# Gates of the first two chunks by seven half-size products, on fp16 sums kept in borrowed space

## The chip, the core and the metric

One core of one Trainium2 chip runs the whole program. The metric is device microseconds (us) of one execution, as the median of several. Engines are named as in the profile: PE (TensorE matmuls), PEld (its weight loads), DVE (VectorE), ACT (ScalarE), POOL (GpSimd), SPq (the queue that issues most transfers).

## The reference, cut to what matters

```python
xn = _layernorm(x)                       # x: 2048 x 448
s  = attention(xn, k_cache, v_cache, wq, wo)          # 16 heads of 256, window 512
g  = silu((gelu(xn @ w_gate) * (xn @ w_up)) @ w_down) # F = 1792; this is the "gate"
out = x + s * g
```

The rows are handled in four chunks of 512. The products with w_gate and w_up (the FFN stage) of all chunks come first, in rounds of two units; a unit is 128 of the 1792 columns F, so a chunk has 14 units and 7 rounds, and "round n" computes units n and n + 1. The product with w_down of a chunk, followed by the silu, is called the gate of that chunk. Only the gates of chunks 0 and 1 lie within the FFN stage; the other two run later, among the attention scores.

## The kernel before: the parts concerned

```python
def gu_evac(n, b):                       # after the matmuls of unit n
    act(gl[:, s, :], bank[b], ACT.Gelu_apprx_tanh, ...)
    K.op("dve", tensor_tensor(actT[:, c % 2, f, :], bank[b + 1], gl[:, s, :], ALU.mult), ...)

def down(c, pairs):                      # the gate of chunk c: eight products
    for t4 in range(4):
        mms([(bank[b][:, 0:D], actT[:, c % 2, f, t4*P:(t4+1)*P], wd[:, f, :], f == 0, f == NF-1)
             for f in range(NF)], ...)
        act(tmp[:, s, 0:D], bank[b][:, 0:D], ACT.Tanh, ..., scale=0.5)
        K.op("dve", ... out=g2w[:, t % NXR, :] ...)     # NXR = 3 buffers
        dma("sp", g2d[t], g2w[:, t % NXR, :], ...)

def ln_norm(t, dup="dve"):
    nm(0, D, 0, b_xn[s][0])              # the 448 columns, on DVE
    if dup == "dve":
        nm(D, DP, K3, b_xn[s][1])        # the last 64 columns once more, on DVE
    else:
        act(xn[:, s, D:DP], xn[:, s, K3:D], ACT.Copy, ...)   # or copied, on ACT

def ln_a(): ...                          # statistics of the next tile (DVE), deviation (POOL)
def ln_b(): ln_norm(ln_t[1]); ln_tp_dma(ln_t[1]); ...

DOWN_AT = {NF + 5: 0, 2 * NF + 1: 1}     # gates of chunks 0 and 1
for n in range(4, NU, 2):                # the rounds
    gu_group((n, n + 1), cur)            # PE
    gu_evac(n, cur[0])
    ln_b()
    gu_evac(n + 1, cur[1])
    if ln_t[0] < 8 or n >= 12: ln_a()
    # ... casts and sums of wo, loads of wq, v, k at n == 32 ...
    if n + 1 in DOWN_AT: down(DOWN_AT[n + 1], cur)
```

VectorE and ScalarE each work through their own list in the order in which the program names the operations (the lines of round 18 below show it: a gelu whose bank was written by 39.52 us started at 42.78, behind the copy named before it). A round writes four PSUM banks and the next round the other four, so PE can start round n + 4 only when the products of round n have been read out (round 22 below waits 0.94 us for one of round 18).

The softmax here doesn't subtract the row's maximum and nothing guards it: scores larger than these inputs give would overflow.

## Time and profile before

| | before |
|---|---|
| median (later 4 runs) | 548.0 us (547.84 to 548.5) |
| PE busy | 98% of the span |
| gate of chunk 0, chunk 1 | 10.70 us each |
| PE idle behind the second gate | 1.23 us |
| one round | 3.02 us |

The prediction below shows the lines of the profile. In its timeline lines the columns are start in us, length in us, engine, source line, operation, output<-inputs, shapes, count, and in brackets the idle time before it with what ended that.

### The profile page before, as it was taken

What the parts mean: (1) busy time and instruction counts of PE and PEld (TensorE: products, weight loads), DVE (VectorE), ACT (ScalarE), POOL (GpSimd) and SP (SyncE); (2) the same over time, 40 slices, a digit from 0 to 9 for tenths busy, and PEclk for the clock granted to TensorE, in tenths of its full rate; (3) what the DMA queues carried; (4) which work ended last, traced back from release to release, by engine and by line L of the source; (5) the groups of instructions that cost most, each with busy time, mean ns of one, the idle gap of its engine ahead of it and who ended that gap; (6) DMA issues with size and microseconds to landing.
All of it is one profiled execution on the core that took longest, in us unless ns stands there. A gap on an engine that the chain in (4) does not pass through costs nothing.

```text
span 545.9 us, 10453 instructions
## 1 busy us (share of the span) xinstructions
PE 537.6 (98%) x3955; PEld 294.5 (54%) x3980; DVE 350.0 (64%) x785; ACT 305.1 (56%) x770; POOL 38.6 (7%) x78
## 2 busy tenths in 40 slices
PE   9999999999999999999999999999999999999997
PEld 5554444445444444894444459644444884444487
DVE  6673726673356757943875786367667934776775
ACT  5433625854448858305875860388578206876820
POOL 1130400000000000003001000020000003001010
PEclk9999999999999999999999999999999999999999
DMA  9568389922264827401771780057546402863731
GB/s 294 122 188 127 65 174 314 206 54 72 74 104 96 151 62 138 95 2 48 168 151 46 151 158 1 18 138 145 104 89 151 79 2 68 165 153 83 151 53 34
DMA packets 171458, 61.34 MB, mean 112 GB/s; under 512 B 154960, under 2 KB 168272, under 8 KB 171408
## 3 DMA queue, kind: packets, MB, share of 16 engines
q1 hardware_dynamic: 167632, 51.39, 44.2%
q0 software_dynamic: 3008, 8.72, 6.6%
q8 instruction: 31, 0.51, 0.4%
q10 hardware_dynamic: 768, 0.57, 0.3%
q14 instruction: 19, 0.16, 0.1%
HBM read 19.76 MB, written 3.67 MB: 43 GB/s over the span
## 4 chain that ended last, share of the span: by engine, by line
PE 93%; DMA 2%; ACT 2%; DVE 2%; issue 1%; DVEq 0%; ACTq 0%
PE bank L357 92%; DMA g_all<-g2w 2%; ACT p L703 1%; PE bank L474 1%; DVE pn L710 1%; ACT qT L348 0%; DVE rden L707 0%; DVE g2w L534 0%; PE bank L455 0%; DVE qT L688 0%; ACT oTh L348 0%; ACT xnT L348 0%; DVE xnT L351 0%; DVE xr L351 0%; DVE gl L387 0%
## 5 line engine op out<-in xcount | busy, mean ns | idle before, releaser
L703 ACT ACTIVATE p<-bank 128x512 f32<-128x512 f32 x256 | 150.5, 596 | 24.3 <-DVE pn L710 19.1
L357 PE MATMUL bank<-pT,va 128*128 128x512 bf16 x512 | 120.8, 379 | 0.0
L357 PE MATMUL bank<-kT,qT 128*128 128x512 bf16 x487 | 117.8, 379 | 2.3 <-ACT qT L348 1.0
L710 DVE TENSOR_SCALAR pn<-p,rden 128x512 bf16<-128x512 f32 x256 | 113.0, 484 | 7.8 <-DMA pT<-pn 3.6
L357 PE MATMUL bank<-xnT,wq 64*128 64x512 bf16 x768 | 94.9, 376 | 0.0
L357 PE MATMUL bank<-xnT,wgu 64*128 64x512 bf16 (+2 forms) x768 | 83.9, 350 | 1.3 <-DVE g2w L534 1.2
L357 PEld LDWEIGHTS bank<-kT,qT 128*128 128x128 bf16 x512 | 49.4, 98 | 62.0 <-issue 3.8
L357 PEld LDWEIGHTS bank<-pT,va 128*128 128x128 bf16 x512 | 50.0, 98 | 60.4 <-DMA pT<-pn 0.9
L348 ACT ACTIVATE qT<-bank 128x512 bf16<-128x512 f32 x76 | 44.1, 596 | 55.4 <-PE bank L357 53.8
L688 DVE CAST qT<-bank 128x512 bf16<-128x512 f32 x52 | 35.1, 692 | 54.7 <-PE bank L357 54.7
L357 PEld LDWEIGHTS bank<-xnT,wq 64*128 64x128 bf16 x768 | 36.7, 94 | 46.3 <-ACT p L703 2.1
L357 PEld LDWEIGHTS bank<-xnT,wgu 64*128 64x128 bf16 x768 | 37.0, 94 | 38.5 <-DVE g2w L534 1.7
L348 ACT ACTIVATE gl<-bank 128x512 bf16<-128x512 f32 x56 | 33.2, 597 | 39.0 <-PE bank L357 36.7
L707 DVE RECIPROCAL rden<-rsum 128x2 f32<-128x2 f32 x128 | 21.2, 166 | 49.6 <-ACT p L703 49.6
L523 DVE TENSOR_TENSOR actT<-bank,gl 128x512 bf16<-128x512 f32 x56 | 37.8, 690 | 21.9 <-PE bank L357 15.6
L703 ACT ACTIVATION_READ_ACCUMULATOR p<-bank 128x1 f32 x256 | 51.7, 202 | 0.0
L357 PE MATMUL bank<-wt,sr 128*128 128x224 f16 x512 | 49.7, 259 | 0.0
L357 PEld LDWEIGHTS bank<-wt,sr 128*128 128x128 f16 x512 | 49.1, 98 | 0.0
L348 ACT ACTIVATE xnT<-bank 128x224 bf16<-128x224 f32 (+2 forms) x12 | 4.4, 400 | 71.7 <-PE bank L357 70.9
L357 PE MATMUL bank<-wd,actT 128*128 128x448 bf16 x224 | 43.0, 353 | 0.0
L728 DVE TENSOR_SCALAR oTh<-bank 128x512 f16<-128x512 f32 x62 | 42.4, 684 | 0.0
L348 ACT ACTIVATE oTh<-bank 128x512 f16<-128x512 f32 x66 | 38.9, 590 | 4.6 <-PE bank L357 4.6
(51 smaller groups left out, 352.1 us busy)
## 6 DMA issues: line engine op xcount, KB each, us to landing
wtb<-in_A_wo_dram POOLq DMA_DIRECT2D x4, 896.0 KB, 10.8
wq<-in_A_wq_dram SPq DMA_DIRECT2D x2, 1536.0 KB, 9.2
va<-in_A_v_cache_dram SPq DMA_DIRECT2D x8, 256.0 KB, 6.3
pT<-pn SPq DMA_TRANSPOSE x128, 2.8
g_all<-g2w SPq DMA_DIRECT2D x16, 112.0 KB, 1.8
xr<-in_A_x_dram POOLq DMA_DIRECT2D x15, 112.0 KB, 2.4
wd<-in_B_w_down_dram SPq DMA_DIRECT2D x1, 1568.0 KB, 7.6
g<-g_all POOLq DMA_DIRECT2D x14, 112.0 KB, 2.3
```

Of the source, the lines that this page charges most:

```text
L348: K.op("act", lambda e, o=o, i=i: e.activation(o, i, func, scale=scale), reads, writes)
L357: ins = e.matmul(o, lhsT=l, rhs=r, start=st, stop=sp, skip_group_check=True)
L474: ins = e.matmul(bank[b][:, 0:w], lhsT=gl[:, 0, 0:P], rhs=gl[:, 0, 0:w], start=True, stop=True)
L523: K.op("dve", lambda e: e.tensor_tensor(actT[:, c % 2, f, :], bank[b + 1], gl[:, s, :], ALU.mult), (b_ps[b + 1], b_gl[s]), (b_actT[c % 2][ ...
L688: K.op("dve", lambda v, s=s, b=b: v.tensor_copy(qT[:, s, 1, :], bank[b + 1]), (b_ps[b + 1],), (b_qT[s][1],))
L703: K.op("act", lambda e, b=b, r=r, z=z: e.activation(p32[:, z, :], bank[b], ACT.Exp, scale=att_scale, accum_out=rsum[:, r:r + 1]), (b_ps[b] ...
L707: K.op("dve", lambda e, r=r: e.reciprocal(rden[:, r - 1:r + 1], rsum[:, r - 1:r + 1]), b_rsum[r - 1:r + 1], b_rden[r - 1:r + 1])
L710: K.op("dve", lambda e, r=r - 1 + t, z=(n - 1 + t) % NP32, y=y, t=t: e.tensor_scalar(pn[:, y, t, :], p32[:, z, :], rden[:, r:r + 1], None, ...
L728: K.op("dve", lambda v, i=i, b=b: v.tensor_scalar(oTh[:, i, :], bank[b], WS, None, op0=ALU.mult), (b_ps[b],), (b_oT[i],))
```

## The change

Its intent: in the gates of chunks 0 and 1, cut the matrices into 2 x 2 blocks and replace the eight products of blocks by seven (Strassen's scheme in Winograd's form), paying with sums of w_down and of the activations on DVE and casts to fp16 on ACT. The sums live in space that k, v and wq need later, so those loads move behind the second gate. The first gate moves from behind round 18 to behind round 26, the second from behind round 28 to behind round 38, and the layernorm of tiles 12 to 15 and the casts and sums of wo to later rounds. In every round with a layernorm, the copy of the last 64 columns moves from VectorE to ScalarE (`"act"`), where it stands between the two gelus. The core of the diff (the seven products and their sums are cut):

```diff
-        b_va = [K.buf() for g in range(Hkv)]
+        b_va = sbuf_bufs(a, NJ * Dh * 2, Hkv)
...
+        g2w = [g2w[:, i, :] for i in range(NXR)] + [g2[:, 0, :]]
+        b_g2w = sbuf_bufs(a, D * 2, NXR) + b_g2[:1]
...
+        wdt, b_wdt, a2 = temp("wdt", [P, 7, NH, N2], F16, b_kT[0].lo, 7)
+        sd, b_sd, a2 = temp("sd", [P, 4, NH, HC], F16, a2, 4)
...
+        def cast_wd(j, e, n, i): ...      # act: w_down to fp16
+        def sum_wd(o, x, y): ...          # dve: 128 x 1568
+        def sum_act(c, k, i): ...         # dve: 128 x 1024 or 128 x 768
+        def down7(c, one, other): ...     # seven products of 14 matmuls, 224 columns
...
         def ln_b():
             if ln_t[1] < ln_t[0]:
-                ln_norm(ln_t[1])
+                ln_norm(ln_t[1], "act")
...
-        DOWN_AT = {NF + 5: 0, 2 * NF + 1: 1}
+        WD_CASTS = [(16, (j, e, n, i)) for j, e, n in (...) for i in range(2)]
+        DN_SUMS = [(n, sum_act, (0, k, i)) for i, n in ((0, 14), (1, 16)) for k in range(4)] + [
+            (20, sum_wd, x) for x in (...)] + [
+            (n, sum_act, (1, k, i)) for i, n in ((0, 28), (1, 30)) for k in range(4)]
+        DOWN_AT = {27: 0, 39: 1}
...
-            if ln_t[0] < 8 or n >= 12:
+            if ln_t[0] < 8 or 12 <= n and ln_t[0] < 12 or n >= 28:
                 ln_a()
...
-            if n == 32:                   # loads of wq, v, k
...
+                cur, nxt = down7(DOWN_AT[n + 1], cur, nxt)
+                if DOWN_AT[n + 1] == 1:   # loads of wq(0), k 0-1, wq(1), v, k 2-7
```

More of the change, by code (lines that the diff above doesn't have):

```diff
@@ L270, in bass_recurrent_scan__sliding_block_cached__geglu_ffn__prompt_kernel @@
         g2w, _, _ = place("g2w", [P, NXR, D], BF16, at=a)
-        b_g2w = sbuf_bufs(a, D * 2, NXR)
+        g2w = [g2w[:, i, :] for i in range(NXR)] + [g2[:, 0, :]]
+        b_g2w = sbuf_bufs(a, D * 2, NXR) + b_g2[:1]
         tmp, a, _ = place("tmp", [P, 2, QC], F32)
@@ L301, in bass_recurrent_scan__sliding_block_cached__geglu_ffn__prompt_kernel @@
         b_actT = [sbuf_bufs(a + i * NF * QC * 2, QC * 2, NF) for i in range(2)]
+        actTh, _, _ = place("actTh", [P, 2, NF, QC], F16, at=a)
         NGL = 3
@@ L304, in bass_recurrent_scan__sliding_block_cached__geglu_ffn__prompt_kernel, with temp @@
         b_gl = sbuf_bufs(a, QC * 2, NGL)
+        NH = NF // 2
+        b_dn = []
+        def temp(name, shape, dt, at, n):
+            t, a, a2 = place(name, shape, dt, at=at)
+            b = sbuf_bufs(a, (a2 - a) // n, n)
+            b_dn.extend(b)
+            return t, b, a2
+        wdt, b_wdt, a2 = temp("wdt", [P, 7, NH, N2], F16, b_kT[0].lo, 7)
+        sd, b_sd, a2 = temp("sd", [P, 4, NH, HC], F16, a2, 4)
+        cd, b_cd, a2 = temp("cd", [P, 3, D], F32, a2, 3)
+        th, b_th, a2 = temp("th", [P, 2, D], F32, a2, 2)
+        g2x, a, a2 = place("g2x", [P, 4, D], BF16, at=at)
+        b_g2x = sbuf_bufs(a, D * 2, 4)
         NPT, NPN, NP32 = 3, 3, 3
@@ L522, in gu_evac @@
             act(gl[:, s, :], bank[b], ACT.Gelu_apprx_tanh, (b_ps[b],), (b_gl[s],))
-            K.op("dve", lambda e: e.tensor_tensor(actT[:, c % 2, f, :], bank[b + 1], gl[:, s, :], ALU.mult),
+            o = actTh if c < 2 else actT
+            K.op("dve", lambda e: e.tensor_tensor(o[:, c % 2, f, :], bank[b + 1], gl[:, s, :], ALU.mult),
                  (b_ps[b + 1], b_gl[s]), (b_actT[c % 2][f],))
@@ L533, in down @@
                 act(tmp[:, s, 0:D], bank[b][:, 0:D], ACT.Tanh, (b_ps[b],), (b_tmp[s],), scale=0.5)
-                K.op("dve", lambda e, t=t, b=b, s=s: e.scalar_tensor_tensor(
-                    out=g2w[:, t % NXR, :], in0=tmp[:, s, 0:D], scalar=1.0, in1=bank[b][:, 0:D],
-                    op0=ALU.add, op1=ALU.mult), (b_tmp[s], b_ps[b]), (b_g2w[t % NXR],))
-                dma("sp", g2d[t], g2w[:, t % NXR, :], (b_g2w[t % NXR],), (b_g2d[t],))
+                K.op("dve", lambda e, t4=t4, b=b, s=s: e.scalar_tensor_tensor(
+                    out=g2w[t4], in0=tmp[:, s, 0:D], scalar=1.0, in1=bank[b][:, 0:D],
+                    op0=ALU.add, op1=ALU.mult), (b_tmp[s], b_ps[b]), (b_g2w[t4],))
@@ new lines, in down, with cast_wd, sum_wd, sum_act @@
+                dma("sp", g2d[t], g2w[t4], (b_g2w[t4],), (b_g2d[t],))
+        def cast_wd(j, e, n, i):
+            fs = (slice(0, 4), slice(4, NH))[i]
+            fe = slice(e * NH + fs.start, e * NH + fs.stop)
+            act(wdt[:, j, fs, :], wd[:, fe, n * N2:(n + 1) * N2], ACT.Copy, (b_wd,), b_wdt[j:j + 1], scale=WS)
+        def sum_wd(o, x, y):
+            add("dve", wdt[:, o, :, :], wdt[:, x, :, :], wdt[:, y, :, :], [b_wdt[x], b_wdt[y]], b_wdt[o:o + 1], ALU.subtract)
+        def sum_act(c, k, i):
+            fs = (slice(0, 4), slice(4, NH))[i]
+            o = lambda e, r: (actTh[:, c, e * NH + fs.start:e * NH + fs.stop, r * HC:(r + 1) * HC],
+                              b_actT[c][e * NH + fs.start:e * NH + fs.stop])
+            S = lambda j: (sd[:, j, fs, :], b_sd[j:j + 1])
+            j, (x, bx), (y, by), op = ((3, o(0, 0), o(0, 1), ALU.subtract), (2, o(1, 1), S(3), ALU.subtract),
+                                       (0, S(2), o(0, 0), ALU.add), (1, o(1, 0), S(2), ALU.subtract))[k]
+            add("dve", S(j)[0], x, y, bx + by, S(j)[1], op)
@@ new lines, in down7, with product, plus, gate @@
+        def down7(c, one, other):
+            B1, B4, B6, B7, B5, B3 = one[0], one[0] + 1, one[1], one[1] + 1, other[0], other[0] + 1
+            F = 1.0 / WS
+            A = lambda e, r: (lambda i: actTh[:, c, e * NH + i, r * HC:(r + 1) * HC], b_actT[c][e * NH:(e + 1) * NH])
+            S = lambda i: (lambda k: sd[:, i, k, :], b_sd[i:i + 1])
+            U2, U3 = tmp[:, 0, 0:D], tmp[:, 1, 0:D]
+            bU2, bU3 = b_tmp[:1], b_tmp[1:]
+            def product(j, b, x, first=True):
+                lhs, bx = x
+                mms([(bank[b][:, t * N2:(t + 1) * N2], lhs(i)[:, t * P:(t + 1) * P], wdt[:, j, i, :],
+                      first and i == 0 and t == 0, False) for i in range(NH) for t in range(2)], bx + [b_wdt[j]], (b_ps[b],))
+            def plus(o, bo, b, V, bV):
+                K.op("dve", lambda e: e.scalar_tensor_tensor(
+                    out=o, in0=bank[b][:, 0:D], scalar=F, in1=V, op0=ALU.mult, op1=ALU.add), [b_ps[b]] + bV, bo)
+            def gate(q, r, n):
+                two = lambda x: x.rearrange("p (t d) -> p t d", t=2)
+                act(th[:, q % 2, :], cd[:, q % 3, :], ACT.Tanh, b_cd[q % 3:q % 3 + 1], b_th[q % 2:q % 2 + 1], scale=0.5)
+                def end():
+                    K.op("dve", lambda e: e.scalar_tensor_tensor(
+                        out=g2x[:, 2 * r:2 * r + 2, n * N2:(n + 1) * N2], in0=two(th[:, q % 2, :]), scalar=1.0,
+                        in1=two(cd[:, q % 3, :]), op0=ALU.add, op1=ALU.mult),
+                        (b_th[q % 2], b_cd[q % 3]), b_g2x[2 * r:2 * r + 2])
+                return end
+            def store(r):
+                for t in range(2 * r, 2 * r + 2):
+                    dma("sp", g2d[c * 4 + t], g2x[:, t, :], (b_g2x[t],), (b_g2d[c * 4 + t],))
+            product(0, B1, A(0, 0))
+            act(U2, bank[B1][:, 0:D], ACT.Copy, (b_ps[B1],), bU2, scale=F)
+            product(5, B6, S(2))
+            product(6, B7, S(3))
+            product(3, B4, A(1, 1))
+            product(4, B5, S(0))
+            product(2, B3, S(1))
+            product(1, B1, A(1, 0), False)
+            plus(U2, bU2, B6, U2, bU2)
+            plus(U3, bU3, B7, U2, bU2)
+            plus(cd[:, 0, :], b_cd[:1], B4, U3, bU3)
+            g0 = gate(0, 1, 0)
+            plus(cd[:, 1, :], b_cd[1:2], B5, U3, bU3)
+            g1 = gate(1, 1, 1)
+            plus(U2, bU2, B5, U2, bU2)
+            g0()
+            plus(cd[:, 2, :], b_cd[2:], B3, U2, bU2)
+            g1()
+            store(1)
+            g2_ = gate(2, 0, 1)
+            act(cd[:, 0, :], bank[B1][:, 0:D], ACT.Copy, (b_ps[B1],), b_cd[:1], scale=F)
+            g2_()
+            gate(3, 0, 0)()
+            store(0)
+            return (other[1], one[1]), (one[0], other[0])
@@ L625, in sum_wt @@
                 [b_wt[x][i], b_wt[y][i]], b_wt[o][i:i + 1], ALU.subtract)
-        CASTS = [(18, (j, i)) for j in (0, 4) for i in range(NB)] + [(40, (j, i)) for j in (2, 1) for i in range(NB)]
-        SUMS = [(32, (4, 4, 0, i)) for i in range(NB)] + [
-            (44, (o, x, y, i)) for i in range(NB) for o, x, y in ((5, 2, 4), (6, 5, 0), (3, 1, 5))]
-        DOWN_AT = {NF + 5: 0, 2 * NF + 1: 1}
+        CASTS = [(24, (j, i)) for j in (0, 4) for i in range(NB)] + [(46, (j, i)) for i in range(NB) for j in (2, 1)]
+        SUMS = [(40, (4, 4, 0, i)) for i in range(NB)] + [
+            (48, (o, x, y, i)) for i in range(NB) for o, x, y in ((5, 2, 4), (6, 5, 0), (3, 1, 5))]
+        WD_CASTS = [(16, (j, e, n, i)) for j, e, n in ((0, 0, 0), (4, 0, 1), (2, 1, 1), (1, 1, 0)) for i in range(2)]
+        DN_SUMS = [(n, sum_act, (0, k, i)) for i, n in ((0, 14), (1, 16)) for k in range(4)] + [
+            (20, sum_wd, x) for x in ((4, 4, 0), (5, 2, 4), (6, 5, 0), (3, 1, 5))] + [
+            (n, sum_act, (1, k, i)) for i, n in ((0, 28), (1, 30)) for k in range(4)]
+        DOWN_AT = {27: 0, 39: 1}
         gu_evac(0, 0)
@@ L652, in bass_recurrent_scan__sliding_block_cached__geglu_ffn__prompt_kernel @@
                 load_wt(4, 0, 1)
-            if n == 30:
+            if n == 36:
                 K.reuse([b for j in (1, 2, 3, 5, 6) for b in b_wt[j]])
@@ L656, in bass_recurrent_scan__sliding_block_cached__geglu_ffn__prompt_kernel @@
                 load_wt(1, 1, 0)
+            for i in range(2):
+                if WD_CASTS and n >= WD_CASTS[0][0]:
+                    cast_wd(*WD_CASTS.pop(0)[1])
+            for i in range(2 if n in (14, 20, 22, 24, 26, 36, 38) else 1):
+                if DN_SUMS and n >= DN_SUMS[0][0]:
+                    _, f, x = DN_SUMS.pop(0)
+                    f(*x)
             for i in range(2 if n >= 40 else 1):
@@ L659, in bass_recurrent_scan__sliding_block_cached__geglu_ffn__prompt_kernel @@
                     cast_wt(*CASTS.pop(0)[1])
-            for i in range(2 if n >= 44 else 1):
+            for i in range(3 if n >= 48 else 1):
                 if SUMS and n >= SUMS[0][0]:
                     sum_wt(*SUMS.pop(0)[1])
-            if n == 32:
-                for g in range(NG):
-                    load_wq(g)
-                for g in range(Hkv):
-                    load_v(g)
-                for g in range(Hkv):
-                    load_k(g)
-            if n + 1 in DOWN_AT:
-                down(DOWN_AT[n + 1], cur)
-                cur, nxt = nxt, cur
+            if n + 1 in DOWN_AT:
+                assert not DN_SUMS or DN_SUMS[0][0] > n
+                cur, nxt = down7(DOWN_AT[n + 1], cur, nxt)
+                if DOWN_AT[n + 1] == 1:
+                    K.reuse(b_kT + b_va)
+                    for b in [y for x in b_wql for y in x]:
+                        b.old.extend(y for x in b_dn for y in x.readers + [x.writer] if y is not None)
+                    load_wq(0)
+                    for g in range(2):
+                        load_k(g)
+                    load_wq(1)
+                    for g in range(Hkv):
+                        load_v(g)
+                    for g in range(2, Hkv):
+                        load_k(g)
         def q_group(n, pairs, more_act=False):
```

## The prediction

> **What bounds the kernel now.** I read the page's busy shares first, then the chain that ended last, then the groups, and last the timeline around the two gates (the products with w_down of chunks 0 and 1) that the change rewrites.
>
> ```profile
> PE 537.6 (98%) x3955; PEld 294.5 (54%) x3980; DVE 350.0 (64%) x785; ACT 305.1 (56%) x770; POOL 38.6 (7%) x78
> ...
> PE 93%; DMA 2%; ACT 2%; DVE 2%; issue 1%; DVEq 0%; ACTq 0%
> ```
>
> PE is busy 98% and carries 93% of the chain, so only two things move the end: matmul time taken out, and idle time of PE put in or taken out. From the timeline of the early stage, the second gate, and from the last burst, which already works with seven products (columns: start, length, engine, line, operation, count, idle before and its releaser):
>
> ```profile
> 63.89 10.77 PE L357 MATMUL bank<-wd,actT 128*128 128x448 bf16 x56
> ...
> 74.59 0.82 PE L357 MATMUL bank<-xnT,wgu 64*128 64x512 bf16 x6
> ...
> 79.20 0.62 DVE L534 SCALAR_TENSOR_TENSOR g2w<-tmp,bank 128x448 bf16<-128x448 f32 x1 [5.84 <-DMA g_all<-g2w]
> ...
> 79.88 0.82 PE L357 MATMUL bank<-xnT,wgu 64*128 64x512 bf16 x6 [1.23 <-DVE g2w L534]
> ```
> ```profile
> 524.09 12.43 PE L357 MATMUL bank<-wt,sr 128*128 128x224 f16 x128
> 536.36 6.30 PE L357 MATMUL bank<-wt,oTh 128*128 128x224 f16 x64
> ```
>
> A gate of eight products takes 74.59 - 63.89 = 10.70 us, 191 ns for each of 56 matmuls. A 224-column matmul of the seven-product kind goes at (536.36 - 524.09)/128 = 95.9 ns. And PE stood still 1.23 us because the last gate step waited for a buffer whose store was slow.
>
> How VectorE and ScalarE follow the FFN matmuls is the other half. One round is two units, and PE needs 3.02 us for it: VectorE's first products of successive rounds start at 20.00 and 23.03 below.
>
> ```profile
> 20.00 0.69 DVE L523 TENSOR_TENSOR actT<-bank,gl 128x512 bf16<-128x512 f32 x1 [0.47 <-PE bank L357]
> 20.61 0.60 DVE L430 TENSOR_SCALAR xn<-x,mv,rstd 128x448 bf16<-128x448 bf16 x2
> 21.12 0.69 DVE L523 TENSOR_TENSOR actT<-bank,gl 128x512 bf16<-128x512 f32 x1
> 21.72 0.62 DVE L404 BATCH_NORM_STATS2 stats<-x 128x6 f32<-128x448 bf16 x1
> 22.38 0.18 DVE L407 BATCH_NORM_AGGREGATE mv<-stats 128x2 f32<-128x6 f32 x1
> 23.03 0.69 DVE L523 TENSOR_TENSOR actT<-bank,gl 128x512 bf16<-128x512 f32 x1 [0.47 <-PE bank L357]
> ```
> ```profile
> L348 ACT ACTIVATE gl<-bank 128x512 bf16<-128x512 f32 x56 | 33.2, 597 | 39.0 <-PE bank L357 36.7 <-DVE stats L404 0.6
> L348 ACT ACTIVATE wt<-wtb 128x896 f16<-128x896 bf16 x16 | 14.7, 942 | 5.6 <-DMA wtb<-in_A_wo_dram 5.6
> L351 DVE TENSOR_TENSOR wt<-wt 128x896 f16<-128x896 f16 x16 | 9.5, 618 | 0.1
> L351 DVE TENSOR_TENSOR sr<-oTh 128x1024 f16<-128x1024 f16 x16 | 10.9, 684 | 0.0
> L430 DVE TENSOR_SCALAR xn<-x,mv,rstd 128x448 bf16<-128x448 bf16 x16 | 6.3, 392 | 0.7 <-POOL rstd L416 0.6
> L348 ACT ACTIVATE xn<-xn 128x64 bf16<-128x64 bf16 x1 | 0.3, 258 | 0.0
> ```
>
> A round with layernorm work leaves VectorE 0.47 us free. The last six lines are the by-shape groups (count, then busy us and mean ns): they price each new operation.
>
> [...]
>
> **The change part by part.**
> 1. *Products.* Chunks 0 and 1 take 7 x 7 x 2 = 98 matmuls of 224 columns instead of 56 of 448: 98 x 95.9 = 9.40 us against 10.70. Saved on PE: 1.30 each, 2.60 in all.
> 2. *Buffers of the gate.* Four own output buffers, and the large loads are issued after the second gate's stores: the stall of 1.23 us goes. Sum of gains: 3.83 us.
> 3. *Loads of wq, k, v.* They start some 2.5 us after the second gate ends, when the last use of the borrowed space is over, instead of at 80.2. Eight rounds (24 us) then pass before the first q product. In the kernel before, the whole sequence was issued in 30 us (80.2 to 110.7); wq's first half, k 0 and k 1 come first in the new order, and v 0 and k 2 are needed tens of us later. I count no stall.
> 4. *New side work.* ScalarE: eight casts of w_down (four of 942 ns, four of 672 elements[...]), two in each of rounds 16, 18, 20, 22: 1.6 us per round with overlap. VectorE: four sums of w_down of 1568 elements (slope (684-618)/128 = 0.52 ns, so 0.97 us each, estimate), and per chunk four sums of 1024 elements (0.69) and four of 768 (estimate 0.55). All of this is beside PE if the rounds stay under 3.02 us.
> 5. *The small copy of the normalized tile goes to ScalarE.* It now stands between the two gelus of a round. It waits for VectorE's normalization, which stands behind the product of the first gelu. So in a round with a normalization the two engines no longer run side by side: gelu 0.60, hand-over 0.07, product 0.61 (start to start, 20.00 to 20.61), normalization 0.39, hand-over 0.06, copy 0.26, gelu 0.60 = 2.59 us. VectorE saves little: both small steps together had taken 21.12 - 20.61 = 0.51.
>
> **The rounds against 3.02 us.** For ScalarE a round with copy and two casts is 2.59 + 1.6 = 4.2. For VectorE, from its first product to its next: 0.61 + 0.39 + (0.06 + 0.26 + 0.60 + 0.07) + 0.61 + statistics 0.84 + one sum 0.69 = 4.1. Round 14, with two dependent sums (1.4), is 4.8; rounds 16 and 18 are 4.2; round 20 is 4.2 by ScalarE. Together 17.4 us where PE needs 12.1: 5.3 late. A product may be late by 3.02 + 0.26 - 0.95 or so before PE misses its bank (it frees the bank 0.95 us after the round; the bank is wanted 3.02 after): 2.1 us of slack. So about 3.3 us of PE idle before the first gate, in rounds 20 to 26. Round 24 (products 1.24 and two large sums 2.0) keeps the lag: VectorE starts round 26 about 2.2 us late, and the sum for the third product is done 0.26 + 2.2 + 1.24 + 0.97 = 4.7 us after the gate starts, wanted at 2 x 1.34 = 2.7: 2.0 us more. First gate: 5.3.
> Chunk 1: rounds 30, 32, 34 are 4.1 by VectorE, 36 is 0.61 + 0.39 + 0.99 + 0.61 + 1.1 = 3.7: 16.0 against 12.1, 3.9 late, 2.1 slack, so about 1.5 of PE idle before the gate, and the second product then waits for the last act sums, about 1.7 more. Second gate: 3.2.
> Sum: -3.8 + 5.3 + 3.2 = +4.7 us, so 552.6.
>
> **Rivals.**
> - *The side work hides* and PE gains all 3.8 us: 544.0. For it: on averages both engines have room, and without the copy's hand-over ScalarE would need 1.2 + 1.6 = 2.8 us per round. Against: the order of the instructions in the built kernel, gelu, copy, gelu, with the copy waiting on VectorE. About one in five.
> - *Half hides*: the lag is smaller than my hand walk says, for instance because back-to-back operations overlap more. Then 546 to 550.
> - *The late loads become the bound*: q or the first scores wait for wq or k, or the score transposes queue behind the loads. Load issue took 30 us and 30 us are there before the first scores; each us over it costs up to 1 us. Then 555 to 560. Against: the order puts first what is needed first. One in fifteen.
>
> **Range and chances.** The sum is 552.6; the errors lie more on the low side (the first two rivals), so I say 551.6, with 545.8 to 555.0. More than 2% faster would need 11 us, three times the whole gain: 1%. More than 2% slower would need stalls of 15 us: 3%.
>
> **What would show it.** Matmuls of 224 columns in the gates at 96 ns: step 1. No wait of PE on the gate's store: step 2. PE idle of 3 to 4 us between rounds 20 and 26 put down to VectorE's product, then idle inside the first gate at its second and third product, released by a sum of w_down: step 5 and the walk. In ScalarE's waits a new row, the small copy waiting for the normalization, about 1.1 us each time. PE over 98% busy before 95 us would prove me wrong; so would idle at the first q product or the first scores (step 3).

## More of the kernel before

One further line is wanted later, the first product of the attention scores, as a mark that stands just behind the FFN stage:

```profile
121.65 1.67 PE L357 MATMUL bank<-kT,qT 128*128 128x512 bf16 x7 [0.16 <-DVE qT L688]
```

## The result, and the profile after

The changed kernel took 551.84 us (median of 4 runs, 551.44 to 553.04) against 548.01 before. The ratio is 1.0072, 95% interval 1.0054 to 1.009. The change costs 0.7%, well clear of the noise but under 2%.

The page's busy shares and its chain by engine, after:

```profile
PE 536.6 (98%) x4039; PEld 299.6 (55%) x4064; DVE 366.9 (67%) x805; ACT 313.2 (57%) x794; POOL 41.7 (8%) x78
...
PE 86%; DVE 5%; ACT 5%; issue 2%; POOL 1%; DMA 1%; DVEq 0%; ACTq 0%
```

PE is still busy 98%, rounded; but the chain that ended last, 93% PE before, now runs through DVE and ACT for a tenth of the span (4% before). The averages hide the change of regime; the chain shows it. The timeline of one round (round 18) shows how the two engines are tied together:

```profile
40.61 0.59 ACT L365 ACTIVATE gl<-bank 128x512 bf16<-128x512 f32 x1
...
41.30 0.69 DVE L541 TENSOR_TENSOR actTh<-bank,gl 128x512 f16<-128x512 f32 x1
...
42.19 0.40 DVE L447 TENSOR_SCALAR xn<-x,mv,rstd 128x448 bf16<-128x448 bf16 x1 [0.20 <-POOL rstd L433]
42.62 0.26 ACT L365 ACTIVATE xn<-xn 128x64 bf16<-128x64 bf16 x1 [1.42 <-DVE xn L447]
...
43.26 1.59 ACT L365 ACTIVATE wdt<-wd 128x896 f16<-128x896 bf16 x2
43.46 0.69 DVE L541 TENSOR_TENSOR actTh<-bank,gl 128x512 f16<-128x512 f32 x1 [0.88 <-ACT gl L365]
...
44.21 0.82 PE L374 MATMUL bank<-xnT,wgu 64*128 64x512 bf16 x6 [0.94 <-DVE actTh L541]
...
44.75 0.59 ACT L365 ACTIVATE gl<-bank 128x512 bf16<-128x512 f32 x1
```

Read it downwards: first gelu, its product on DVE, the normalization, the copy on ACT (which had stood idle 1.42 us for it), the second gelu (42.78, though the 18 matmuls that ended its bank and began round 20 were over by 39.52), then casts; DVE meanwhile waits 0.88 us for that second gelu. ACT's rounds start 44.75 - 40.61 = 4.14 us apart where PE needs 3.02, and PE waits 0.94 us for a product. The gates, after:

```profile
53.63 1.52 PE L374 MATMUL bank<-wdt,actTh 128*128 128x224 f16 x14
...
57.35 1.51 PE L374 MATMUL bank<-wdt,sd 128*128 128x224 f16 x14 [0.57 <-DVE wdt L368]
...
64.17 0.82 PE L374 MATMUL bank<-xnT,wgu 64*128 64x512 bf16 x6
```
```profile
83.63 1.52 PE L374 MATMUL bank<-wdt,actTh 128*128 128x224 f16 x14
86.56 2.86 PE L374 MATMUL bank<-wdt,sd 128*128 128x224 f16 x28 [1.41 <-DVE sd L368]
...
94.72 0.82 PE L374 MATMUL bank<-xnT,wgu 64*128 64x512 bf16 x6
```

The first gate lasts 64.17 - 53.63 = 10.54 us and the second 94.72 - 83.63 = 11.09, although 98 matmuls at 95.9 ns are 9.40: both wait inside for sums. The first scores start at 125.26, against 121.65 before: 3.61 us later. From there to the end it is 424.4 us in the changed kernel and 424.2 before. So all of the loss of these two executions happens in the FFN stage.

### The profile page after: what moved, and what is told of

It is laid out like the page before. It is cut to its first block, busy times and chain, and to the rows that moved or that the text cites. A ratio compares the mean times of both kernels' runs of the same rounds, so it can differ in the third digit from the quotient of the medians.

```text
span 549.7 us, 10673 instructions
## 1 busy us (share of the span) xinstructions
PE 536.6 (98%) x4039; PEld 299.6 (55%) x4064; DVE 366.9 (67%) x805; ACT 313.2 (57%) x794; POOL 41.7 (8%) x78
## 4 chain that ended last, share of the span: by engine, by line
PE 86%; DVE 5%; ACT 5%; issue 2%; POOL 1%; DMA 1%; DVEq 0%; ACTq 0%
PE bank L374 85%; ACT gl L365 2%; DVE actTh L541 1%; ACT p L814 1%; PE bank L491 1%; DVE stats L421 1%; ACT qT L365 1%; POOL rstd L433 1%; DVE xn L447 1%; DMA pT<-pn 1%; POOL ve L431 1%; DVE pn L821 1%; ACT wdt L365 0%; ACT xn L365 0%; DVE actT L541 0%
## 5 line engine op out<-in xcount | busy, mean ns | idle before, releaser
L374 PEld LDWEIGHTS bank<-xnT,wgu 64*128 64x128 bf16 x768 | 34.8, 94 | 43.6 <-DVE actTh L541 5.1
L374 PE MATMUL bank<-wt,oTh 128*128 128x224 f16 x384 | 38.3, 259 | 0.3 <-ACT oTh L365 0.3
L374 PEld LDWEIGHTS bank<-wt,oTh 128*128 128x128 f16 x384 | 36.7, 98 | 1.8 <-ACT oTh L365 1.1
```

Of the source, the lines that this page charges most:

```text
L374: ins = e.matmul(o, lhsT=l, rhs=r, start=st, stop=sp, skip_group_check=True)
```

## The experiments

Eight kernels ran, all timed in five rounds (five or six executions each) and all correct. "Before" below is the kernel before on the same chip in the same rounds.

**e1: the copy back on VectorE.**

```diff
-                ln_norm(ln_t[1], "act")
+                ln_norm(ln_t[1])
```

> The changed kernel, with the small copy of the normalized tile back on VectorE; all else as changed. Hand-over theory (the copy between the two gelus couples ScalarE and VectorE): a VectorE round with layernorm and one sum is 0.61 + 0.51 + 0.61 + 0.84 + 0.61 = 3.2 us instead of 4.1 and a ScalarE round with two casts 2.8 instead of 4.2, so the lag stays under the slack of 2.1 us; PE idle before both gates and in the second falls to about 0, in the first about 0.5 us stays; about 544.7 us, 0.6% faster than the kernel before. Amount theory (there is simply too much side work): VectorE gets more work, so 552 or more. Late-loads theory (wq, k, v come too late): unchanged, 551.8.

Measured: 544.31 us (544.04 to 544.74), before 547.75; ratio 0.9936 (0.9924 to 0.9948). One word turns a loss of 0.7% into a gain of 0.6%. ACT's rounds in this run, and the start of the first gate and of the scores:

```profile
37.48 1.25 ACT L365 ACTIVATE gl<-bank 128x512 bf16<-128x512 f32 x2 [0.28 <-PE bank L374]
38.62 1.59 ACT L365 ACTIVATE wdt<-wd 128x896 f16<-128x896 bf16 x2
40.50 1.25 ACT L365 ACTIVATE gl<-bank 128x512 bf16<-128x512 f32 x2 [0.29 <-PE bank L374]
```
```profile
50.11 1.51 PE L374 MATMUL bank<-wdt,actTh 128*128 128x224 f16 x14
...
118.04 1.67 PE L374 MATMUL bank<-kT,qT 128*128 128x512 bf16 x7 [0.16 <-DVE qT L799]
```

The two gelus run back to back again, the rounds are 3.02 us apart, and ACT even waits for PE. The first gate starts at 50.11, where the kernel before, without any idle, would have come to 37.98 + 4 x 3.02 = 50.06. The amount theory (there is simply too much side work) expected 552 or more and falls, for the very same side work is there.

**e2: the copy stays on ScalarE, last in its round.**

```diff
-                ln_norm(ln_t[1], "act")
-                ln_tp_dma(ln_t[1])
+                ln_norm(ln_t[1], "later")     # the 448 columns only
+                late_copy.append(ln_t[1])
...
                     cast_wt(*CASTS.pop(0)[1])
+            ln_copy()                         # copy on ACT and transpose, here
```

> The changed kernel with the copy kept on ScalarE, but issued as the last thing of its round, behind both gelus and the casts. Hand-over theory: the normalization is long done by then, ScalarE's round is 1.2 + 1.6 + 0.2 = 3.0 us and VectorE's 3.1, so nearly all of the idle time goes: 544.5 to 546 us. If what costs is the copy's own time on ScalarE or the amount of side work: 551 to 552 as in the changed kernel. Late-loads theory: 551.8.

Measured: 550.26 us (549.11 to 551.93), before 547.75; ratio 1.0044 (1.0029 to 1.006). Taken by its time, it speaks against the hand-over theory (that the copy between the gelus ties the two engines together). The timeline of PE says otherwise:

```profile
32.23 1.46 PE L374 MATMUL bank<-xnT,wgu 64*128 64x512 bf16 x6 [2.97 <-DVE mv L424]
...
35.50 0.82 PE L374 MATMUL bank<-xnT,wgu 64*128 64x512 bf16 x6
```

PE idles once for 2.97 us, before the first group of chunk 1, and then runs at half speed until 35.50: six matmuls take 1.46 us instead of 0.82, and the granted clock (the share of TensorE's full speed that it was given) over this stretch was 0.52. From 31.00 to 32.20, the last part of the wait, it already averaged 0.91. Of e2's six executions five show a mean granted clock of 0.996 or 0.997 and one 1.0, so the fall did not come every time. From 35.50 on there is no stall to speak of before or in the gates: the first gate starts at 55.03, 4.97 us behind 50.06, of which the wait and the half clock over 3.3 us make about 4.6. VectorE is named as the releaser only because its record came last; what that group needs is the transposed tile 7, and by the order of the queue its transpose (issued at 24.67) now stood behind the 1.5 MB load of w_down, issued at 22.90. This was a flaw of the edit, so the run's time decides nothing, and e5 mends it.

**e5: the same, with the early copies ahead of that load.**

```diff
             gu_evac(n + 1, cur[1])
+            if n < 14:
+                ln_copy()
```

> The run with the copy last in its round lost nearly all its time at one place, 2.97 us of PE idle before the first group of chunk 1 and slow matmuls behind it: there the transpose of tile 7 had come to stand behind the 1.5 MB load of w_down in the queue, which is a flaw of my edit. Here the copy and its transpose stand ahead of that load in the rounds before 14, and at the end of the round from 14 on. Hand-over theory: 544.3 to 545.3 us, as with the copy on VectorE, and no idle of PE before or inside the gates. If the copy on ScalarE costs as such: 549 or more.

Measured: 544.73 us (544.13 to 545.18), before 547.93; ratio 0.9938 (0.9926 to 0.9951), the same as e1 within the intervals. The one wait of 2.97 us is gone, which fits the reading of e2. ACT's lines of the same stage:

```profile
40.47 0.26 ACT L365 ACTIVATE xn<-xn 128x64 bf16<-128x64 bf16 x1
40.80 1.24 ACT L365 ACTIVATE gl<-bank 128x512 bf16<-128x512 f32 x2
```

The copy takes the same 0.26 us on the same engine but waits for nothing. So neither the engine nor the length of the copy costs anything that these times show; its place does.

**e3: the kernel before with that part of the change alone.** The same word, in the kernel before (`ln_norm(ln_t[1], "act")`).

> The kernel before with one part of the change alone: the copy on ScalarE between the gelus. Hand-over theory: rounds with layernorm grow to 3.4 us by VectorE and 3.5 by ScalarE, over 3.02, but only by 0.4 to 0.5 each, so most goes into the slack of 2.1 us; the changed kernel's trace lost about 0.8 us before round 14 already, which should be seen here too: 548.8 to 549.3 us. Amount theory: VectorE has less work and gains or stays: 547.9 to 548.0.

Measured: 550.60 us (550.27 to 550.98), before 547.75; ratio 1.0052 (1.0039 to 1.0065). The direction was right and the size was not: 2.9 us, not 0.8 to 1.3. VectorE's lines between the gates of this run, from the second product of one round to the second product of the next:

```profile
58.86 0.69 DVE L523 TENSOR_TENSOR actT<-bank,gl 128x512 bf16<-128x512 f32 x1 [0.88 <-PE bank L357]
59.47 0.62 DVE L404 BATCH_NORM_STATS2 stats<-x 128x6 f32<-128x448 bf16 x1
...
60.22 0.67 DVE L523 TENSOR_TENSOR actT<-bank,gl 128x512 bf16<-128x512 f32 x1
61.37 0.40 DVE L430 TENSOR_SCALAR xn<-x,mv,rstd 128x448 bf16<-128x448 bf16 x1 [0.48 <-POOL rstd L416]
62.64 0.69 DVE L523 TENSOR_TENSOR actT<-bank,gl 128x512 bf16<-128x512 f32 x1 [0.88 <-ACT gl L348]
```

The second products stand at 55.08, 58.86, 62.64 and 66.42: 3.78 us apart to the hundredth, where I had counted 3.44. The second product of each round stands before the statistics; those go to GpSimd for the deviation, and the next normalization waits 0.48 us for it. With the copy between the gelus this closes a loop through three engines: statistics, deviation (GpSimd), normalization, copy (ACT), second gelu (ACT), second product, next statistics. I had walked the round without GpSimd in it.

**e8: that loop opened.**

```diff
         def ln_b():
-            if ln_t[1] < ln_t[0]:
+            if ln_t[1] < ln_t[0] - (ln_t[1] >= 8 and ln_t[0] < NT):
                 ln_norm(ln_t[1], "act")
```

> The run with the copy alone on ScalarE lost 2.9 us instead of the 0.8 to 1.3 I expected, and its rounds repeat every 3.78 us, not 3.44: each closes a loop through GpSimd (statistics, reciprocal deviation there, normalization, copy, second gelu, second product, next statistics), with 0.48 us of VectorE waiting for GpSimd. Here, for tiles 8 to 15, the normalization takes the tile whose statistics are two rounds old instead of one, so that loop is open. If the loop through GpSimd is the cause of the miss: rounds of about 3.44 us, wait on GpSimd gone there, about 0.8 us lost in the early rounds (which stay as they are) and up to 0.5 later: 548.6 to 549.3 us. If it is not: 550.6 as before.

Measured: 550.32 us (549.2 to 550.81, 6 runs), before 547.92; ratio 1.0043 (1.0031 to 1.0055). The total missed the expected 548.6 to 549.3. The stage concerned did what was expected and more (rounds of 3.44 us were expected); two second products of successive rounds:

```profile
54.78 0.69 DVE L523 TENSOR_TENSOR actT<-bank,gl 128x512 bf16<-128x512 f32 x1 [0.88 <-ACT gl L348]
...
57.99 0.69 DVE L523 TENSOR_TENSOR actT<-bank,gl 128x512 bf16<-128x512 f32 x1 [0.88 <-ACT gl L348]
```

The rounds are 3.21 us apart, and the wait on GpSimd is gone there. The second gate, in e3 and then in e8:

```profile
67.17 10.77 PE L357 MATMUL bank<-wd,actT 128*128 128x448 bf16 x56 [1.45 <-DVE actT L523]
```
```profile
65.16 10.77 PE L357 MATMUL bank<-wd,actT 128*128 128x448 bf16 x56 [0.25 <-DVE actT L523]
```

From the start of the first gate (38.88 and 38.92) to that of the second it is 28.29 us in e3 and 26.24 in e8, against 25.91 before. So the loop is shown as the cause of 2.05 of the 2.38 us that e3 lost between its gates. (The first scores start at 121.52, 2.77 us sooner than in e3, 124.29. The rest of that, 0.7, is not the loop: e3 still waited 0.58 us behind the second gate for its store, and e8's trace shows no such wait.)

But the total did not follow: from the first scores to the end this run took 425.9 us, against 424.1 to 424.4 in the traces of e1, e3, e4, e5, e7, the changed kernel and the one before. In that part PE waited 1.3 us in all for transposes of the probabilities, and one of them took 4.95 us on the chain. Why they were slower in this kernel, whose later part has the same code, stays open. The traces of e2 (424.9) and e6 (425.4, where PE waited 0.8 us for such transposes) are longer in that part too, so it may be a spread between executions; but the trace is of the fastest of e8's six, so that would not explain its median of 550.32.

**e4: the kernel before with the four gate buffers of the change.** The two lines `g2w = ...` and `b_g2w = ...` of the diff, and their use, in the kernel before.

> The kernel before with four output buffers for the gate instead of three (the fourth is the first buffer of the later gate reads, as in the change). My step 2: PE's wait of 1.23 us behind the second gate goes: 546.8 us. Rival: the slow store (11 us) delays something else, for instance the loads behind it, and nothing is gained: 548.0.

Measured: 546.29 us (546.05 to 546.61), before 547.75; ratio 0.9972 (0.996 to 0.9984). In its trace PE waits nowhere for the gate's store, and the first scores start at 120.48, 1.17 us earlier:

```profile
120.48 1.67 PE L358 MATMUL bank<-kT,qT 128*128 128x512 bf16 x7 [0.16 <-DVE qT L689]
```

Step 2 is worth what it promised, and it does not need the seven products.

**e6: the changed kernel with the loads held back.**

```diff
-                if DOWN_AT[n + 1] == 1:
-                    K.reuse(b_kT + b_va)
+            if n == 42:
+                    K.reuse(b_kT + b_va)
+                    for b in b_kT + b_va + [y for x in b_wql for y in x]:
+                        b.old.append(b_actT[1][1].writer)   # product of unit 43
```

> The changed kernel with the loads of wq, k and v held back until the second unit of the round after next is evicted, about 5 us later than in the changed kernel. Late-loads theory (they bind): 5 us longer, 556 to 557. Mine: in the changed kernel the loads were all issued by 128.6 us and what stands behind them in the queue was wanted only near 140, so nothing moves: 551.5 to 552.3.

Measured: 552.29 us (551.29 to 552.74), before 547.93; ratio 1.0076 (1.0063 to 1.0088), the changed kernel's own 1.0072 within the interval. The queue's timeline, its last kT transposes, in the changed kernel and then in this run:

```profile
118.89 9.75 SPq L362 DMA_TRANSPOSE kT<-in_A_k_cache_dram  x6
```
```profile
123.70 10.40 SPq L362 DMA_TRANSPOSE kT<-in_A_k_cache_dram  x6
```

The loads end 5.5 us later (134.1 against 128.6) and PE waits for none of them. The late-loads theory, which expected 556 to 557, falls.

**e7: e1, with the statistics of tiles 8 to 11 two rounds earlier** (`8 <= n` in place of `12 <= n` in the condition of `ln_a`).

> The changed kernel with the copy on VectorE and, besides, the statistics of tiles 8 to 11 two rounds earlier (rounds 8 to 14 instead of 12 to 18), to take the last 0.16 us of waiting out of the first gate. 544.0 to 544.4: at best 0.2 us under the run with the copy alone, possibly nothing measurable.

Measured: 543.87 us (543.7 to 544.03), before 547.93; ratio 0.9924 (0.991 to 0.9937). This is the best version: 0.76% faster than the kernel before and 1.5% faster than the changed one. Its interval overlaps that of e1, so the extra gain is not shown by the times; in its trace both gates last 9.4 us, with no idle of PE from unit 4 to the first q products.

## Why the prediction was right, point by point

The time, 551.84 us, came out 0.2 us from the prediction of 551.6. That closeness is luck; the sum before discounting said 552.6 (from 548.0 it would be 552.7), and the terms below erred in both directions. Its terms, in us, by the two traces:

| term | predicted | in the trace |
|---|---|---|
| products, two gates | -2.60 | -2.60 (98 x 95.9 ns; see below) |
| wait behind the second gate | -1.23 | -1.23 |
| idle in the rounds before 14 | 0 | +0.83 |
| idle in rounds 14 to 26 | +3.3 | +2.7 |
| idle inside the first gate | +2.0 | +1.1 |
| idle in rounds 28 to 38 | +1.5 | +1.3 |
| idle inside the second gate | +1.7 | +1.7 |
| sum | +4.7 | +3.8 |

How the right column is worked out: the first gelu of round 14 starts at 32.22, against 31.39 before: 0.83. The gate would have started at 50.06 + 0.83 = 50.89 and started at 53.63: 2.7. The gates lasted 10.54 and 11.09 instead of 9.40: 1.1 and 1.7. Six rounds after 64.17 are 82.29, and the second gate started at 83.63: 1.3. The sum of 3.8 agrees with the 3.61 seen at the first scores.

- *Step 1, products.* Right. In e1, where almost nothing else is in the way, the gates last 9.55 and 9.40 us (last product's start plus 1.34), and the first scores come 120.48 - 118.04 = 2.44 us earlier than in e4, which has the same buffers but eight products. The medians of the two differ by 2.0.
- *Step 2, the buffer wait.* Right, shown alone by e4.
- *Step 3, the loads.* Right, shown by e6: they had about 5 us to spare.
- *Step 4, side work.* The estimated operations came out as worked out: a w_down sum took 969 ns (estimate 0.97 us), the smaller sums about 550 (0.55). The casts took 944 and 756; a straight line through the 258 ns for 64 columns and 942 for 896 in the trace before gives 758 for 672. Two casts in a row took 1.59 us (1.6 in the prediction, an estimate), 0.11 less than 0.944 + 0.756.
- *Step 5, the copy.* Right, and shown three ways: moved to VectorE (e1), moved to the end of its round (e5), and alone in the kernel before (e3). The rounds of 4.2 us by ScalarE measured 4.14. The hand-overs of 0.06 and 0.07 were estimates; in round 18 it is 0.03 from the normalization's end to the copy (42.59 to 42.62) and 0.10 from the second gelu's end to its product (43.36 to 43.46). The sign that was named is there: the copy waited for the normalization 12 times, 21.3 us in all, so 1.8 each where 1.1 had been said. VectorE did save little: in e5's trace the normalization without the small step holds it 0.30 us (36.60 to 36.90), against the prediction's 0.51 for both.
- *What was mis-sized.* The rounds before 14 were counted as free and cost 0.83 us; e3 has the same early rounds and starts its first gate 0.9 us late. In two of the changed kernel's three normalizations there VectorE waited 0.48 us for GpSimd's deviation. The first gate's idle was overrated (2.0 for 1.1). The two errors partly cancelled. The slack of 2.1 us, an estimate, is also not what the prediction's own terms give (3.02 + 0.26 - 0.95 = 2.33); with 2.33 the idle before the first gate would be 5.3 - 2.33 = 3.0, nearer to the 2.7 measured. The step that left GpSimd out of the round hardly mattered here, as with sums in the round most of that wait lies under VectorE's work (0.20 us in the lines above), but it made the expectation for e3 (0.8 to 1.3 us, measured 2.9) too small by a factor of two to three.
- *The rivals.* "The side work hides" was wrong for the change as made, though its number, 544.0, is about what e1, e5 and e7 reach (544.3, 544.7, 543.9) once the copy is out of the way. "Half hides" (546 to 550) did not come true either. "The late loads become the bound" fell with e6.

## What to carry to other kernels

When two in-order engines hand work back and forth inside a loop, put an operation that waits for the other engine at the end of its round, not between two operations that the other engine waits for; 0.26 us of work per round in the wrong place cost 1.3% here. Judge such a move by walking the round through every engine that is in the cycle, including the one that is busy 8% of the time, and compare the sum with the round of the engine that bounds. And try the parts of a change one by one: the seven products were worth having, and one word of the same diff hid that.
